# Low parts of three weight units summed by the matrix engine, one softmax in two blocks, taps for two groups at once, and a new order

## The chip, the cores and the metric

The kernel runs on one core of a Trainium2 chip. The metric is device time in microseconds (us). PE is the matrix engine (PEld its weight loads), DVE the vector engine, ACT the scalar engine, POOL the GpSimd engine and SP the engine that issues every DMA here. Each engine works through its own queue in program order and stops at an instruction whose inputs, or whose place to write to, aren't ready.

## The reference, cut to what matters

```python
# q, k, v: (8, 8, 576, 64); nine chunks of 64 keys per sequence
scores = scale * (q_c @ k_c.T)                      # within a chunk
attn = exp(scores - max(scores)); attn = attn / (sum(attn) + 1e-9)
x = (attn @ v_c)                                    # laid out as (8, 576, 512)
gate_pre[t] = sum over k of conv_w[k] * x[t - 4 + k]   # five taps along the sequence, causal
gate = 1 / (1 + exp(-gate_pre))
out = (gate * (x @ w_val)) @ w_out
```

The two weight matrices and the taps arrive as 64-bit floats. All sums are kept near float32 precision: each factor of the two large products is split in a high part and a low part (float32r, the one-pass format of PE), and a product is high·high + high·low + low·high.

## The kernel before, in words

The 4608 tokens are cut in nine groups of 512; groups 0 to 7 hold one sequence's first 512 tokens each and group 8 the last 64 of all eight. Channels stand on the partitions, 512 channels in four tiles of 128. A *pair* (g, p) is one half of a group's heads; its tiles are 128 x 1024.

The string `ORDER` lists the work piece by piece, and every piece is a short function that issues one to 64 instructions. They stand in each engine's queue in that order; nothing else schedules them. All go through the helper `run` (line 130), so the profile shows one line for all; the tiles tell them apart. `SLOTS` lists which buffer each new tile takes (`z`: 38 of 128 x 1024; `b`: four PSUM tiles of 128 x 2 x 512; `e`: two for exponentials). A piece that takes a buffer waits until everything that read its former content is done.

The pieces that matter here:

- `lq`, `lk`, `lv`, `lw`, `lc`: loads (SP). A `w_val` *unit* (`v 0` to `v 3`) is 256 rows by 256 columns, 512 KB.
- `w1` to `w8`, `wa`, `wb`: from 64-bit words to parts. `w1`, `w3`, `w4`, `w7` (DVE), `w2`, `w5` (ACT) pick exponent, sign and mantissa; `wq` is then the leading float32 of a weight and `wr` (made by `w8`, POOL, or `w8D`, DVE) the rest. `w6` (ACT) rounds `wq` to the high part `v_hi`; `wa` computes `wq - v_hi` and `wb` adds `wr`, which gives the low part `v_lo`. A `D` at a name's end moves a piece to DVE.
- `S` (PE): scores of one half (b) of a pair, 16 products of 64 x 64, into PSUM. `mx` (DVE): row maxima. Then either `sb`, `ex`, `sm` (subtract on DVE, one exponential of 128 x 1024 on ACT, sum and reciprocal on DVE) or `ng`, `ea`, `rc`: `ea` is 16 exponentials of 128 x 64 on ACT, with the maximum as bias, each followed by the read of its sum.
- `nm` (POOL): multiply by the reciprocal. `T` (PE): eight transposes by the identity. `ec` (ACT): copy from PSUM. `A` (PE): weighted sum of v. `xr` (ACT): high part of x; `xd` (DVE): low part; `xc` (ACT): x itself.
- `V g m c t` (PE): one term of x·w_val, 512 columns, for output tile m and input tile c (c = 2, 3 belong to pair 1; c = 2 is its first half, c = 3 its second). Term 0 is high·high, 1 uses `v_lo`, 2 the low part of x. `vc` copies the result.
- `k0` (ACT), `k` (DVE): the first and the other four taps, 128 x 512 each. `sg` (ACT): sigmoid. `gs` (DVE): gate times value; `gr` (ACT), `gd` (POOL or DVE): its high and low part. `P g t c` (PE): three terms of the last product. `oc`, `st`: copy and store.
- `W n` (PE): n products of zeros, 128 x 512, that nobody reads; they keep PE busy before its real work is there.

The program opens with the loads, the four `w_val` units and the softmax of the pairs (0, 1), (0, 0) and (1, 0). PE's long work starts with the first `V`, which needs x of pair (0, 1).

Of the kernel before, what the change touches and what calls it, by code (L numbers as in the profile page):

```python
# [66 lines left out]
sg 3 1,k 3 1 4,V 7 3 1,k 6 1 1,P 4 3 1,sg 3 0,k 6 3 3,V 6 0 3,gs 3 1,P 4 1 3,vc 6 0,V 7 3 0,nmD 8 1,P 4 1 2,P 4 3 2,k 7 0 1,
V 7 2 3,k 7 1 2,gs 3 0,P 4 0 2,vc 7 1,P 4 0 3,k0D 5 2,gr 3 1,P 4 1 1,nmD 8 0,gr 3 0,P 4 1 0,k 6 2 2,P 4 3 0,gd 3 0,P 4 0 1,
T 8 1,oc 4 0,T 8 0,ecD 8 1,hc 6 0,P 4 2 2,hc 3 0,gd 3 1,ecD 8 0,P 4 2 3,P 3 2 0,oc 4 1,A 8 0,k0 7 3,hc 7 0,k0D 5 3,hc 5 1,
hc 6 1,hc 0 0,k 5 0 2,A 8 1,hc 4 1,hc 7 1,xr 8 0,hc 5 0,k 6 3 4,P 3 2 1,xc 8 1,xd 8 0,P 3 3 0,k 6 1 2,P 3 3 3,xc 8 0,  # L70
V 8 0 0,k 6 1 3,hb 0,P 3 2 3,hb 1,k 7 3 1,k0 8 2,V 8 1 0,k 6 1 4,xr 8 1,k 6 2 3,V 7 0 0,sg 6 0,xd 8 1,V 7 1 3,P 3 3 1,
k0 8 3,k 8 2 1,P 3 2 2,k 5 0 3,P 3 3 2,k0D 8 0,V 8 0 3,k 6 2 4,oc 3 1,k 5 3 1,V 7 0 1,k0 8 1,k 7 3 2,P 3 0 0,sg 6 1,k 5 0 4,
P 3 0 3,k 5 2 1,V 8 2 0,gs 6 1,P 3 1 2,P 3 1 3,k 5 2 2,gr 6 1,P 3 1 0,k 7 1 3,V 8 2 1,k 5 1 4,P 3 1 1,k 7 0 2,sg 5 0,
# [22 lines left out]
    b="0 0 1 1 2 0 2 2 1 2 1 3 1 0 2 1 1 0 2 1 2 3 3 0 2 1 0 1 0 2 1 0 1 3 1 0 0 1 3 2 0 2 0 0 2 1 3 0 2 2 0 1 3 0 2 "  # L96
      "1 2 2 0 2 1 3 1 0 2 2 2 1 1 0 3 0 2 3 1 3 0 2 3 1 3 1 0 2 1 3 0 3 2 0 1 3 1 0 1 2 3 1",
    e="0 1 1 1 1 0 1 0 1 0 1 0 1 0 1 0 0 1",
)


@with_exitstack
def chunk_attention_gated_conv(ctx, tc, q, k, v, w_val, conv_w, w_out, out):
# [5 lines left out]
    P = 128  # L109
# [417 lines left out]
```

## Time and profile before

| | |
|---|---|
| three runs | 282.32, 285.37, 285.33 us; median 285.33 |
| the profiled execution | 282.82 us, of which the span from first to last instruction is 281.0 |
| busy, share of the span | PE 96%, DVE 87%, PEld 77%, ACT 71%, POOL 23% |
| granted PE clock, mean | 0.994 |
| moved by DMA | 42.47 MB, mean 151 GB/s; some 400 GB/s over the first 60 us |
| chain that ended last | PE 92%, DMA 4%, ACT 2% |

Busy times say how long an engine had an instruction in work, and PE's are modelled where they overlap; the start-to-start distance of neighbours in the timeline is the better price of one. The chain that ended last is followed back from the last instruction, at each step to what released it.

### The profile page before, as it was taken

The page shows a single profiled execution, that of the slowest core. Times are in us where ns is not written, and L with a number is a line of the kernel's source. Part 1 is how long each engine was busy: PE and PEld are TensorE (multiplying, and loading weights), DVE is VectorE, ACT ScalarE, POOL GpSimd, SP SyncE. Part 2 cuts the span into 40 slices and gives each one's busy share as a digit, 9 for nine tenths or more (in the row PEclk, how much of TensorE's full clock was granted, in tenths as well). Part 3 has the DMA queues.
Part 4 walks back from the last instruction along what each step waited for, and adds up shares of the span by engine and source line. Part 5 has one row for each costly group of instructions (what it writes and reads, how often), then busy time and mean ns, then how long its engine had stood idle before and what let it go on. Part 6 is the DMA issues. An engine that isn't in the chain of part 4 may idle for free.

```text
span 281.0 us, 7884 instructions
## 1 busy us (share of the span) xinstructions
PE 270.3 (96%) x3358; PEld 216.2 (77%) x3358; DVE 244.9 (87%) x335; ACT 200.2 (71%) x390; POOL 63.7 (23%) x58
## 2 busy tenths in 40 slices
PE   6498999999999999999999999999999999999995
PEld 2256787887888888888888888888888888887885
DVE  3998999998999798999997999989799999999301
ACT  3686999999889897798798778795595524625011
POOL 1225520461530049160250001100630000210000
PEclk9979999999999999999999999999999999999999
DMA  7999999992010595029055000000000000072156
GB/s 237 355 411 410 409 406 407 378 363 82 9 69 0 204 348 203 3 89 364 2 184 195 0 2 5 0 0 0 2 3 0 0 2 1 0 286 90 77 201 245
DMA packets 15267, 42.47 MB, mean 151 GB/s; under 512 B 1536, under 2 KB 1792, under 8 KB 15232
## 3 DMA queue, kind: packets, MB, share of 16 engines
q1 hardware_dynamic: 15232, 41.97, 39.8%
q8 instruction: 26, 0.43, 0.6%
q14 instruction: 9, 0.07, 0.1%
HBM read 32.53 MB, written 9.44 MB: 149 GB/s over the span
## 4 chain that ended last, share of the span: by engine, by line
PE 92%; DMA 4%; ACT 2%; issue 1%; SPq 0%; ACTq 0%
PE b L130 92%; DMA z<-in_k 3%; DMA z<-in_moe_w_val 2%; ACT z L130 2%; SPq L130 0%; ACTq L130 0%
## 5 line engine op out<-in xcount | busy, mean ns | idle before, releaser
L130 ACT COPY z<-b 128x1024 f32<-128x1024 f32 (+1 forms) x64 | 63.4, 1006 | 50.4 <-PE b L130 50.1
L130 PE MATMUL b<-z,v_hi 128*128 128x512 f32 x288 | 97.4, 401 | 0.1
L130 PE MATMUL b<-o_hi,z 128*128 128x512 f32 (+1 forms) x296 | 96.5, 392 | 0.0
L130 DVE SCALAR_TENSOR_TENSOR z<-z,cw,z 128x509 f32<-128x509 f32 (+3 forms) x128 | 88.6, 743 | 0.1
L130 PEld LDWEIGHTS b<-o_hi,z 128*128 128x128 f32 x296 | 55.1, 188 | 12.5
L130 PEld LDWEIGHTS b<-z,v_hi 128*128 128x128 f32 x288 | 53.9, 188 | 13.4 <-ACT z L130 0.7
L130 PE MATMUL b<-o_lo,z 128*128 128x512 f32 (+1 forms) x148 | 57.5, 388 | 0.0
L130 PE MATMUL b<-z,v_lo 128*128 128x512 f32 x144 | 56.1, 395 | 0.0
L130 PEld LDWEIGHTS b<-z,z 64*64 64x64 f32 x2304 | 36.2, 135 | 15.3 <-issue 9.4
L130 PE MATMUL b<-z,z 64*64 64x64 f32 x2304 | 39.7, 220 | 6.3 <-DMA z<-in_k 3.0
L130 POOL TENSOR_TENSOR z<-z,z 128x1024 fp32r<-128x1024 f32 (+1 forms) x10 | 21.0, 2103 | 101.1 <-ACT z L130 95.4
L130 DVE TENSOR_TENSOR z<-z,z 128x1024 f32<-128x1024 f32 (+2 forms) x33 | 37.0, 1138 | 2.2 <-ACT z L130 1.7
L130 POOL TENSOR_TENSOR z<-e_row,rs 128x1024 f32<-128x1024 f32 x13 | 24.7, 1906 | 55.1 <-DVE rs L130 36.1
L130 ACT ACTIVATE z<-z 128x1024 f32<-128x1024 f32 (+2 forms) x33 | 28.8, 892 | 10.5 <-DVE z L130 10.4
L130 PEld LDWEIGHTS b<-o_lo,z 128*128 128x128 f32 x148 | 27.8, 188 | 5.7
L130 PEld LDWEIGHTS b<-z,v_lo 128*128 128x128 f32 x144 | 27.1, 188 | 5.6
L130 ACT ACTIVATE e_row<-b,mx 128x64 f32<-128x64 f32 x96 | 28.6, 359 | 3.5 <-DVE cw_r L130 2.4
L130 DVE TENSOR_TENSOR z<-b,z 128x1024 fp32r<-128x1024 f32 (+1 forms) x19 | 23.0, 1219 | 3.6 <-ACT z L130 3.4
L130 ACT ACTIVATION_READ_ACCUMULATOR e_row<-b,mx 128x1 f32 x96 | 24.1, 251 | 0.0
L130 ACT CAST z<-z 128x1024 fp32r<-128x1024 f32 x18 | 18.7, 1047 | 5.8 <-DVE z L130 4.8
L130 DVE TENSOR_REDUCE mx<-b 128x16 f32<-128x1024 f32 x18 | 21.3, 1194 | 0.0
L130 DVE COPY z<-b 128x1024 f32<-128x1024 f32 (+2 forms) x8 | 7.8, 989 | 15.2 <-PE b L130 15.2
(50 smaller groups left out, 221.1 us busy)
## 6 DMA issues: line engine op xcount, KB each, us to landing
z<-in_v SPq DMA_DIRECT2D x18, 512.0 KB, 8.3
z<-in_q SPq DMA_DIRECT2D x16, 512.0 KB, 9.9
z<-in_k SPq DMA_DIRECT2D x16, 512.0 KB, 8.4
out<-z SPq DMA_DIRECT2D x16, 512.0 KB, 3.8
z<-in_moe_w_val SPq DMA_DIRECT2D x4, 512.0 KB, 6.2
z<-in_moe_w_out SPq DMA_DIRECT2D x4, 512.0 KB, 10.6
z<-in_k SPq DMA_DIRECT2D x4, 256.0 KB, 6.3
z<-in_q SPq DMA_DIRECT2D x4, 256.0 KB, 6.0
```

The costliest lines, as they stand in the source:

```text
L130: return tc.keep_in_program_order(fn(*args, **kwargs))
```

## The change

**Low parts on PE.** For the units v 1, v 3 and v 2 a piece `Q` (three PE products into PSUM: identity times `wq`, minus identity times `v_hi`, identity times `wr`) and a piece `wc` (ACT copy that rounds to `v_lo`) take the place of `wa` and `wb`. Unit v 0 keeps `wa` and `wb`. A new tile `signed` holds plus and minus identity; ACT fills it (`zs`).

**Two blocks.** For pair (0, 1) the halves of the scores have a PSUM tile each, and `mx`, `ng`, `ea`, `rc`, `nm`, `T`, `ec`, `A`, `xr`, `xd`, `xc` run for one half and then for the other, with half the elements (eight exponentials each instead of 16).

**Two groups at once.** Buffers 20 to 37 become one tile `ys`, so that two of them can be addressed with one stride. `kk` applies a tap to two neighbouring groups in one DVE instruction of 128 x 2 x 508 to 511 (24 of them, for groups 4 with 5 and 6 with 7), `kx` the first tap.

**Fillers.** `W 9 25` (nine products of 512 columns and 25 of 64) at the start replaces `W 14`, `W 7`, `W 9`, `W 1` and `W 3`.

**Order.** The unit v 1 is loaded first and v 3, v 2 ahead of the first k and q; nearly every piece has another place; the buffers are assigned anew.

```diff
-ORDER = """zw,lw v 3,zr 0,zr 1,lw v 1,lc,lk 0 1 0,lq 0 1 0,lq 0 1 1,lk 0 1 1,lw v 2,w1 v 3,...
+ORDER = """zw,lw v 1,zr 1,zr 0,lc,zi,zs 0,zs 1,lw v 3,lw v 2,lk 0 1 0,lq 0 1 0,lq 0 1 1,lk 0 1 1,lq 0 0 0,w1 v 1,...
...
+ALONE = 20
...
+    ys = pool.tile([P, 1 + max(int(i) for i in SLOTS["z"].split()) - ALONE, 2 * T], F32, name="ys")
...
+    signed = pool.tile([P, 2, P], F32R, name="signed")
...
+    def wq_sum(n, c):
+        w_ps[n, c] = unit(bank()[:, 0], n)
+        for i, (lhsT, rhs) in enumerate(((ident, wq[n, c].bitcast(F32)), (signed[:, 1], kept_in(wh, n, c)),
+                                         (signed[:, 0], wr[n, c].bitcast(F32R)))):
+            run(E.matmul, w_ps[n, c], lhsT=lhsT, rhs=rhs if i == 1 else unit(rhs, n), start=i == 0, stop=i == 2)
+
+    def wc(n, c, copy=S.copy):
+        run(copy, out=kept_in(wl, n, c), in_=w_ps[n, c])
...
     def sc(g, p, b):
-        if b == 0:
-            s_ps[g, p] = bank().rearrange("p h (b c k) -> p h b c k", b=2, c=4)
+        own = (g, p) in HALVES
+        if own or b == 0:
+            ps = bank().rearrange("p h (b c k) -> p h b c k", b=2, c=4)
+            if own:
+                s_ps[g, p, b] = ps[:, :, 0]
+            else:
+                s_ps[g, p] = ps
...
+    def ea(g, p, b=None):
+        e = e_of(g, p, b)
+        rss[g, p, b] = r = count("rs")
+        s, m = scores(g, p, b), mxs[g, p, b]
+        for j in range(16 if b is None else 8):
+            eo, si = (e[:, j], s[:, j]) if b is None else (e[:, j // 4, j % 4], s[:, j // 4, j % 4])
+            run(S.activation, out=eo, in_=si, func=AF.Exp, bias=m[:, j:j + 1], scale=SCALE, accum_out=r[:, j:j + 1])
...
+    def two(at, g, hp, a, b):
+        i, j = sorted((at[g, hp // 2][0], at[g + 1, hp // 2][0]))
+        c = hp % 2 * T
+        return ys[:, i - ALONE:j + 1 - ALONE:j - i, c + a:c + b]
...
+    def kk(g, hp, j):
+        d, e = step(xs_at, g, hp // 2), step(acc_at, g, hp // 2)
+        if d * e < 0:
+            tap(g, hp, j)
+            tap(g + 1, hp, j)
+            return
+        a, x = two(acc_at, g, hp, j, T), two(xs_at, g, hp, 0, T - j)
         run(V.scalar_tensor_tensor, out=a, in0=x, scalar=cw[:, hp, TAPS - 1 - j:TAPS - j], in1=a, op0=ALU.mult, op1=ALU.add)
...
-    def keep_warm(n):
+    def keep_warm(n, short=0):
         ps = bank()
-        for _ in range(n):
-            run(E.matmul, ps[:, 0], lhsT=warm[:, :P], rhs=warm, start=True, stop=True)
+        for i in range(n + short):
+            c = slice(0, T if i < n else D)
+            run(E.matmul, ps[:, 0, c], lhsT=warm[:, :P], rhs=warm[:, c], start=True, stop=True)
```

Three places of the queues are spoken of below. First PE's queue up to its first `V` (the rows with `v_hi` or `v_lo` and a z tile, which holds the high part of x). Before, behind `T 0 1` and three fillers, `A` of pair (0, 1) is the row with `z_182`, `T` of (0, 0) the row with `ident`:

```order
L130 MATMUL b_343<-z_333,z_182 64x64 x32
L130 MATMUL b_389<-ident,z_384 128x128 x8
L130 MATMUL b_403<-z_386,v_hi 128x512
L130 MATMUL b_403<-z_386,v_lo 128x512 x2
L130 MATMUL b_403<-z_386,v_hi 128x512 x3
L130 MATMUL b_415<-z_406,z_378 64x64 x32
L130 MATMUL b_452<-z_184,z_376 64x64 x32
```

And in the change, where the rows with `ident` and 128x512 or `signed` are `Q` of v 3 and v 2, `b_309` is `T` of the two halves of (0, 1) with `S 1 0` between them, `b_366` and `b_388` are `A` of the halves:

```order
L139 MATMUL b_291<-z_118,signed 128x512
L139 MATMUL b_299<-z_163,ident 128x512
L139 MATMUL b_299<-v_hi,signed 128x512
L139 MATMUL b_299<-z_168,signed 128x512
L139 MATMUL b_309<-ident,z_297 128x128 x4
L139 MATMUL b_317<-z_192,z_198 64x64 x32
L139 MATMUL b_309<-ident,z_297 128x128 x4
L139 MATMUL b_366<-z_335,z_203 64x64 x16
L139 MATMUL b_388<-z_335,z_203 64x64 x16
L139 MATMUL b_409<-ident,z_383 128x128 x8
L139 MATMUL b_423<-z_386,v_hi 128x512
L139 MATMUL b_425<-z_386,v_hi 128x512
```

The same pairs' pieces stand ahead of the first `V` in both; the fillers between them are gone, and two `Q` stand ahead of the first transposes. PSUM tile number 2 serves `S 0 0`, then `T 0 1`, then `A` of the second half.

Second, ACT's queue from the exponentials of (0, 1) on. Before:

```order
L130 ACTIVATE e_row_63,rs_194<-b_126,mx_180 128x64 x16
L130 CAST v_hi<-z_192 128x2x256
L130 ACTIVATE z_266<-z_88 128x512
L130 ACTIVATE z_299<-z_149 128x512
L130 ACTIVATE z_259<-z_259 128x512
L130 ACTIVATE e_row_64<-e_row_64 128x16x64
L130 COPY z_333<-b_321 128x1024
L130 CAST z_386<-b_343 128x2x2x256
L130 COPY z_400<-b_343 128x2x2x256
L130 COPY z_406<-b_389 128x1024
```

In the change, with `COPY z_335<-b_309` for `ec` of a half, `CAST v_lo` for `wc` and `CAST z_386` for `xr` of a half:

```order
L139 ACTIVATE e_row_65,rs_281<-b_205,mx_236 128x64 x8
L139 ACTIVATE e_row_66<-e_row_66 128x16x64
L139 COPY z_335<-b_309 128x512
L139 CAST v_lo<-b_291 128x2x256
L139 ACTIVATE z_306<-z_306 128x512
L139 CAST v_lo<-b_299 128x2x256
L139 COPY z_335<-b_309 128x512
L139 CAST z_386<-b_366 128x512
L139 COPY ys<-b_366 128x512
L139 ACTIVATE z_407<-z_194 128x512
L139 CAST z_386<-b_388 128x512
L139 COPY ys<-b_388 128x512
```

Between the first `ec` and the first `xr` there was nothing; now two `wc`, a `w2` and the second `ec` stand there, and the copy of `T 0 0` (`ec 0 0`) comes behind all rows shown.

Third, DVE's queue near the end, where the two-group taps stand (rows with 128x2x):

```order
L139 TENSOR_TENSOR z_2989<-ys,z_2979 128x1024
L139 SCALAR_TENSOR_TENSOR ys<-ys,cw 128x2x509 x2
L139 SCALAR_TENSOR_TENSOR z_2842<-tails_74,cw,z_2842 128x512
L139 SCALAR_TENSOR_TENSOR ys<-ys,cw 128x2x509 x2
L139 SCALAR_TENSOR_TENSOR ys<-ys,cw 128x2x508 x3
L139 TENSOR_TENSOR z_3044<-ys,z_2916 128x1024
```

Before, the taps of single groups stood there:

```order
L130 TENSOR_TENSOR z_3096<-z_2645,z_3038 128x1024
L130 SCALAR_TENSOR_TENSOR z_2802<-z_2241,cw,z_2802 128x509
L130 SCALAR_TENSOR_TENSOR z_2677<-z_2531,cw,z_2677 128x510
L130 SCALAR_TENSOR_TENSOR z_2802<-z_2241,cw,z_2802 128x508
L130 SCALAR_TENSOR_TENSOR z_2671<-z_2628,cw,z_2671 128x508
```

All 24 `kk` are one instruction each: the rows with 128x2x508 to 128x2x511 number 24, and those of a single group fell from 128 to 80.

More of the change, by code (lines that the diff above doesn't have):

```diff
@@ L283, in ea, with blocks @@
-    def ea(g, p):
-        probs[g, p] = e_rows[int(next(slots["e"]))]
-        rss[g, p] = r = count("rs")
-        s, m = flat(s_ps[g, p]), mxs[g, p]
-        for j in range(16):
-            run(S.activation, out=probs[g, p][:, j, 0:D], in_=s[:, j], func=AF.Exp, bias=m[:, j:j + 1], scale=SCALE,
-                accum_out=r[:, j:j + 1])
-    def rc(g, p):
-        r = rss[g, p]
+    def blocks(a, b):
+        return a if b is None else a.rearrange("p (h b c) k -> p h b c k", h=2, b=2)[:, :, b]
@@ new lines, in scores, with stat, wide, cols @@
+    def scores(g, p, b):
+        return s_ps[g, p].rearrange("p h b c k -> p (h b c) k") if b is None else s_ps[g, p, b]
+    def stat(a, b):
+        return a if b is None else a[:, 0:8].rearrange("p (h c) -> p h c", h=2)
+    def wide(a, b):
+        return a.unsqueeze(2).broadcast_to([P, 16, D]) if b is None else stat(a, b).unsqueeze(3).broadcast_to([P, 2, 4, D])
+    def cols(a, b):
+        return a if b is None else a[:, 0:8]
+    def mx(g, p, b=None):
+        mxs[g, p, b] = count("mx")
+        run(V.tensor_reduce, out=stat(mxs[g, p, b], b), in_=scores(g, p, b), op=ALU.max, axis=AX.X)
@@ new lines, in e_of, with sb, ex, sm @@
+    def e_of(g, p, b):
+        if not b:
+            probs[g, p] = e_rows[int(next(slots["e"]))]
+        return blocks(probs[g, p][:, :, 0:D], b)
+    def sb(g, p, b=None):
+        run(V.tensor_tensor, out=e_of(g, p, b), in0=scores(g, p, b), in1=wide(mxs[g, p, b], b), op=ALU.subtract)
+    def ex(g, p, b=None):
+        e = blocks(probs[g, p][:, :, 0:D], b)
+        run(S.activation, out=e, in_=e, func=AF.Exp, scale=SCALE)
+    def sm(g, p, b=None):
+        rss[g, p, b] = r = count("rs")
+        run(V.tensor_reduce, out=stat(r, b), in_=blocks(probs[g, p], b), op=ALU.add, axis=AX.X)
+        run(V.reciprocal, out=cols(r, b), in_=cols(r, b))
@@ L293, in rc @@
+    def rc(g, p, b=None):
+        r = cols(rss[g, p, b], b)
         run(V.tensor_scalar, out=r, in0=r, scalar1=1e-9, scalar2=None, op0=ALU.add)
         run(V.reciprocal, out=r, in_=r)
-    def nm(g, p, on=G):
-        normed[g, p] = z().rearrange("p (b k) -> p b k", k=D)
-        run(on.tensor_tensor, out=normed[g, p], in0=probs[g, p][:, :, 0:D], in1=wide(rss[g, p]), op=ALU.mult)
-    def tr(g, p):
-        et_ps[g, p] = bank()
-        to = et_ps[g, p].rearrange("p h (j q) -> p (h j) q", q=P)
-        for j in range(8):
-            run(E.transpose, out=to[:, j, :], in_=normed[g, p][:, 2 * j:2 * j + 2, :].rearrange("p b k -> p (b k)"), identity=ident)
@@ L306, in ec, with nm, tr @@
-    def ec(g, p, copy=S.copy):
-        probs_t[g, p] = z()
-        run(copy, out=twin(probs_t[g, p]), in_=et_ps[g, p])
-    def av(g, p):
-        et = probs_t[g, p].rearrange("p (h b a q) -> p h b a q", h=2, b=2, a=2)
+    def nm(g, p, b=None, on=G):
+        if not b:
+            normed[g, p] = z().rearrange("p (b k) -> p b k", k=D)
+        run(on.tensor_tensor, out=blocks(normed[g, p], b), in0=blocks(probs[g, p][:, :, 0:D], b), in1=wide(rss[g, p, b], b), op=ALU.mult)
+    def tr(g, p, b=None):
+        if not b:
+            et_ps[g, p] = bank()
+        to = et_ps[g, p].rearrange("p h (j q) -> p (h j) q", q=P)
+        for h in range(2):
+            for f in range(2) if b is None else (b,):
+                for a in range(2):
+                    j = 4 * h + 2 * f + a
+                    run(E.transpose, out=to[:, j if b is None else 4 * f + 2 * h + a, :],
+                        in_=normed[g, p][:, 2 * j:2 * j + 2, :].rearrange("p b k -> p (b k)"), identity=ident)
@@ L312, in av, with ec @@
+    def ec(g, p, b=None, copy=S.copy):
+        if not b:
+            probs_t[g, p] = z()
+        if b is None:
+            run(copy, out=twin(probs_t[g, p]), in_=et_ps[g, p])
+        else:
+            run(copy, out=twin(probs_t[g, p])[:, b], in_=et_ps[g, p][:, b])
+    def av(g, p, own=None):
+        et = probs_t[g, p].rearrange("p (h b a q) -> p h b a q" if own is None else "p (b h a q) -> p h b a q", h=2, b=2, a=2)
         vv = vt[g, p].rearrange("p (b h a w d) -> p b h a w d", b=2, h=2, a=2, w=2)
-        x_ps[g, p] = bank()
@@ L452, in zi, with zs_ @@
         make_identity(nc, ident)
+    def zs_(i):
+        run(S.mul, signed[:, i], ident, 1.0 - 2.0 * i)
     def zw():
```

263 lines of the change are left out of this document (140 added, 123 removed), and 12 rows, old and new, of the table z.

## The prediction

> **What bounds the kernel now.** I read the chain of work that ended last first, in order of time (start, length, what). Its longer pieces from 13.8 us on are nearly all PE's:
>
> ```profile
> 13.78 6.14 PE b L130 x135
> 25.15 1.95 ACT z L130 x2
> 27.14 37.07 PE b L130 x795
> 64.21 0.70 issue
> 64.91 12.94 PE b L130 x87
> 79.27 198.80 PE b L130 x2158
> ```
>
> From 27.1 us to 278.1 us PE waits for 0.70 us in one place and about 1.4 us around 78 us in the chain's terms, where PE itself shows hardly a gap. The second view is the timeline of PE at the program's start (start, length, instruction, count, idle before):
>
> ```profile
> 9.15 0.69 PE L130 MATMUL b<-z,z 64*64 64x64 f32 x32 [0.64 <-DMA z<-in_k]
> 9.78 1.68 PE L130 MATMUL b<-warm 128*128 128x512 bf16 x7
> 13.78 1.51 PE L130 MATMUL b<-z,z 64*64 64x64 f32 x64 [2.32 <-DMA z<-in_k]
> 15.22 3.61 PE L130 MATMUL b<-warm 128*128 128x512 bf16 x9
> 20.80 1.06 PE L130 MATMUL b<-ident,z 128*128 128x128 f32 x8
> 25.31 0.50 PE L130 MATMUL b<-z,v_hi 128*128 128x512 f32 x1
> 27.14 2.10 PE L130 MATMUL b<-z,z 64*64 64x64 f32 x128 [0.16 <-ACT z L130]
> 29.17 0.50 PE L130 MATMUL b<-z,v_hi 128*128 128x512 f32 x1
> 36.72 1.78 PE L130 MATMUL b<-z,v_hi 128*128 128x512 f32 x7
> ```
>
> The first `V` stands at 25.31; neighbours of this kind then come every 0.23 us (1.78 us less one overlap, over seven). So the time is made of three things: the start up to the first `V`, some 252 us of dense PE work, and 2.9 us of last copy and store behind 278.1. The change leaves the real PE work behind the first `V` as it is: the same pieces stand ahead of it in both, and the number of products is equal. What it can win is the start, and what it can lose are new waits later. The third view, busy time by stretch (PE, PEld, DVE, ACT, POOL, clock), says who could make PE wait:
>
> ```profile
> 40.00:60.00 20.00, 20.00 (x445) 16.29 (x447) 19.34 (x29) 19.66 (x50) 6.97 (x4) 1.00 1.01 391
> 80.00:100.00 20.00, 20.00 (x240) 16.44 (x229) 18.41 (x29) 18.59 (x50) 3.73 (x3) 1.00 0.28 105
> 240.00:260.00 20.00, 20.00 (x88) 16.08 (x87) 19.35 (x20) 10.05 (x10) 2.68 (x1) 1.00 0.35 132
> 260.00:270.00 10.00, 10.00 (x46) 8.19 (x45) 2.72 (x3) 1.02 (x1) 0.00 (x0) 1.00 0.41 157
> ```
>
> DVE is almost as full as PE up to 260 us, and ACT up to 60. A start that is shorter by x pulls every later date of DVE forward by x too.
>
> **The start, step by step.** The rows for it, DVE, ACT and POOL:
>
> ```profile
> 10.16 1.22 DVE L130 TENSOR_REDUCE mx<-b 128x16 f32<-128x1024 f32 x1
> 18.39 1.23 DVE L130 TENSOR_TENSOR e_row<-b,mx 128x1024 f32<-128x1024 f32 x1
> 20.73 1.24 DVE L130 TENSOR_REDUCE rs<-e_row 128x16 f32<-128x1040 f32 x1
> 11.69 0.32 ACT L130 ACTIVATE e_row<-b,mx 128x64 f32<-128x64 f32 x1 [2.40 <-DVE cw_r L130]
> 16.24 0.30 ACT L130 ACTIVATION_READ_ACCUMULATOR e_row<-b,mx 128x1 f32 x1
> 19.64 1.06 ACT L130 ACTIVATE e_row<-e_row 128x1024 f32<-128x1024 f32 x1 [0.96 <-DVE e_row L130]
> 21.95 1.01 ACT L130 COPY z<-b 128x1024 f32<-128x1024 f32 x1 [1.25 <-PE b L130]
> 24.24 1.01 ACT L130 CAST z<-b 128x1024 fp32r<-128x1024 f32 x1 [1.28 <-PE b L130]
> 26.96 0.64 ACT L130 CAST v_hi<-z 128x512 fp32r<-128x512 f32 x1
> 17.42 1.91 POOL L130 TENSOR_TENSOR z<-e_row,rs 128x1024 f32<-128x1024 f32 x1 [6.05 <-DVE rs L130]
> 24.04 1.27 POOL L130 TENSOR_TENSOR z<-z,z 128x512 f32<-128x512 f32 x1 [1.81 <-DMA z<-in_moe_w_out]
> ```
>
> Sixteen exponentials take 11.69 to 16.54, 0.29 us per step, so eight take 2.3. For a half block I take 0.6 of DVE's 1.22, 1.0 of POOL's 1.91 and 0.55 of ACT's 1.01; a half can't cost more than the whole, so each lies between half a row and a row, and the half plus a little is nearest to the 0.64 us of a 128x512 cast.
>
> - Loads: 512 KB more of weights stand ahead of the first k and q. Between PE's starts at 9.15 and 13.78, 1.5 MB landed, 3.1 us per MB, so the second half of the scores starts at about 10.7 instead of 9.15; the first at about 9.3. What `S 0 0` needs is the same number of bytes as before: 13.7.
> - First half: maxima from 10.1 (DVE is through with two units' bits then), exponentials 11.0 to 13.3. Second half behind one cast: 13.9 to 16.2, against 16.54 before. Splitting saves little there, since ACT does the same 16.
> - DVE next does maxima and subtraction of (0, 0), 14.9 to 17.2 (its scores come at 14.8), then the second reciprocal at 18.0. POOL: the rest of v 2 (1.27) to 14.6, first multiply to 15.6, second 18.1 to 19.1.
> - First transposes: their PSUM tile holds the scores of (0, 0) until 17.2. So they end at about 17.7 if PE is there, against 21.9 before.
> - ACT in its new order: the exponential of (0, 0) 17.3 to 18.35, `ec` 18.9, `wc` 19.45, `w2` 20.0, `wc` 20.6, second `ec` 21.1, `xr` 21.7. Against 25.25 before, where `T`, `ec`, `A`, `xr` followed each other for the whole pair.
> - The sum of (0, 0) on DVE 18.45 to 19.95, its multiply on POOL to 21.9 (before it was on DVE), its transposes to 22.9. They stand ahead of the first `V`, which so starts at about 22.9: **2.4 us earlier.**
> - Then five `V` (1.2 us) until 24.1; `A 0 0` needs `ec 0 0`, which ACT reaches behind `xc`, `w5`, second `xr` and `xc`: 23.85 to 24.8. PE stalls 0.8 us (0.16 before). `A 0 0` and `S 1 1` then end at 26.95, against 29.17 before, with five `V` done instead of six: **2.0 us gained**, if PE's `Q` are out of the way in time.
>
> **What Q costs.** The trace has no 128x512 product in plain float32. The nearest row is the transpose: eight of 128 columns in 1.06 us less an overlap of 0.25, 0.10 us for 128 columns, so 0.41 us for 512; and every 64x64 product of the program is two PE instructions (2304 for 1152 in the queue), so up to 0.81. With two one-pass products of 0.23 a `Q` is 0.87 to 1.3 us; I take 1.3. The Trainium skill, FP8 and Floating Point Precision, section TensorE Precision Notes, counts four passes for true FP32; with 0.23 us per pass that would be an estimate of 0.93 + 0.46 = 1.4 us. `Q` of v 1 is done in PE's idle time at 7 us. Those of v 3 and v 2 stand behind `S 0 0` (14.8): to 17.4 at full clock, just in time for 17.2 above. What they take off DVE and POOL (two `wb`, one `wa` on DVE, 0.6 us each as half of a 1.22 row, three of 1.3 on POOL) is paid by `wc`, 0.55 each, on ACT, where it lies between `ec` and `xr`; it is in the dates above.
>
> But the clock isn't full there. Granted clock by microsecond (PE busy, count, clock, DMA):
>
> ```profile
> 12.00:13.00 1.00, 0.00 (x0) 1.00 1.05 406
> 15.00:16.00 1.00, 1.00 (x13) 0.50 1.02 408
> 17.00:18.00 1.00, 1.00 (x4) 0.50 1.10 438
> 18.00:19.00 1.00, 1.00 (x17) 0.85 0.97 389
> ```
>
> PE idled from 11.46 to 13.78, and from about 14.9 to 18.3 the clock was half: nine fillers took 3.61 us (0.40 each) where seven took 1.68 (0.24), which is 1.45 us lost, on fillers alone. In the change the idle time at 8 to 13.7 us is longer, for the fillers at 9.78 are gone, and the half clock falls on `Q` of v 3 and v 2: 2.6 us each. If it lasts until 18.3, the first is done at 18.5, the second at 19.8, the transposes at 20.3. ACT stands at `ec` from 18.35, and all behind it moves by 2.0 us: **nothing is left of the 2.0.** Whether the gate falls on `Q` depends on where its period lies; I take half of the loss, so a gain of 1.0 with bounds 0 and 2.0.
>
> The rule on this is the Trainium skill's TensorE: Matmul & The Clock Gate, section Part 1: after an idle window of some 3.4 us the clock is halved, a busy one restores it, and the window runs free of the program. The trace agrees: half clock for about 3.4 us. By it the removal of 25 long fillers is a risk, a rival below.
>
> **Later.** Behind `S 1 1` I added up the queues to the first gate products of group 1, since there DVE is nearest. From the sum of (1, 0), which ends at 27.45 by the dates above, to `gdD 1 0` DVE has 39 taps (0.67), 27 instructions of 1024 columns (1.16 apart), four sums with reciprocal (1.5), 22 of 512 columns (0.36 to 0.61) and 7 small ones: 75.1 us. PE has, from 26.95 to `P 1 0 0`, 235 products (0.2325), 8 `T` (0.85), 6 `A` (1.09) and 14 halves of `S` (0.55): 75.7, and 1% for changing between kinds, 76.6. So DVE is there at 102.5, PE at 103.5. To `gdD 1 1` it is 109.2 against 110.0 by the same count. That leaves 0.8 to 1.0 us for all of DVE's waits on the way. In the row 80 to 100 above DVE is idle 1.6 us of 20, so PE will wait; before, the tightest of these places left
>
> ```profile
> 122.02 2.42 POOL L130 TENSOR_TENSOR z<-z,z 128x1024 fp32r<-128x1024 f32 x1 [8.42 <-ACT z L130]
> 124.71 0.50 PE L130 MATMUL b<-o_hi,z 128*128 128x512 f32 x1
> ```
>
> 0.27 us. Bounds of a new stall: 0 and 3.5 (all that DVE idled between 30 and 100 us); I take 1.0, for half of that idling was DVE waiting for PE. The old stall of 0.70 counts as half removed, 0.4.
>
> **Two groups at once** is priced at nothing. Rows for it:
>
> ```profile
> 113.74 5.36 DVE L130 SCALAR_TENSOR_TENSOR z<-z,cw,z 128x511 f32<-128x511 f32 x8
> L130 DVE TENSOR_TENSOR z<-z,z 128x1024 f32<-128x1024 f32 x17 | 20.6, 1221 | 0.9 <-ACT z L130 0.9
> ```
>
> Two taps cost 1.34 us, one instruction of twice the length 1.14 to 1.34 (the second row less the overlap of neighbours). At most 24 x 0.2 = 4.8 us go off DVE, all in groups 4 to 7. There PE is the bound, and DVE is done by 260 us with PE's last 18 us still to come, so this is only slack. If an odd stride cost more than two taps, that slack covers some 5 us. The tail is unchanged: the last store is again 128 KB behind a 128x256 copy.
>
> **Sum**, on the profiled execution: 282.82 - 1.0 (start) - 0.4 (old stall) + 1.0 (new stalls at the gates) = 282.4. Two of the three runs lie 2.5 us above that execution, which one trace can't explain; I add half of that spread: **283.6 us**, against the median of 285.33. A difference under 2% (5.7 us) is about what a measurement of this kernel can't tell from no change.
>
> **Rivals**, on the same scale (before would be 284.1 on it):
>
> - *The start is kept in full.* `Q` run at full clock and DVE, with less to do for the units, is in time: -2.0 - 0.9 and no new stall, 281.2. For it speaks that DVE and POOL lose six instructions at the start; against it the half clock in the rows.
> - *The clock makes it slower.* Without fillers PE is busy for little more than half of 18.3 to 22.9, so the clock falls again and the first `V` run at half: another 1.45 us as for the nine fillers, nothing gained at the start, and 1.0 at the gates: 284.1 + 2.45 = 286.5. It decides once the clock's low stretch reaches past 22.9. By the skill's clock-gate rule this needs a window that counts as idle; the trace shows one with 2.3 us of idling, none with less.
> - *DVE paces groups 1 and 2.* All 3.5 us of its idling come back as PE stalls before 125 us: 284.1 - 1.4 + 3.5 = 286.2. For it: 0.27 us before. Against: half of that idling was caused by PE.
> - *The two-group taps aren't joined* (the code falls back to two taps when the buffers' strides have opposite signs): the queue shows all 24 joined, so no chance is given to it.
>
> **How the numbers follow.** Forecast 0.5, full gain 0.2, clock 0.17, DVE 0.13. The unknown costs move the forecast by -2.4 to +2.5 and the runs' spread by 1.3 either way; with the rivals the range is 279.5 to 287.5. Faster by over 2% (below 279.6) needs the full gain and a low run: 0.1. Slower by over 2% (above 291.0) needs clock and DVE together: 0.06. Within 2%: 0.84.
>
> **What would show it.** The first `V` between 22.9 and 25.3 us; the half clock on a product with `ident` of 128x512, and the first `ec` late by as much; a gap of PE before its products of group 1; DVE's taps of 2 x 509 at 1.14 to 1.34 us; the last product 2.9 us before the end. A first `V` before 22, PE stalls of over 3 us in one place, or a PE gap after 130 us would prove me wrong.

## The result and the profile after

The changed kernel took 287.81 us, median of 7 runs (286.48 to 288.78); the kernel before beside it 283.82 (282.32 to 285.37). The ratio is 1.0129, 95% interval 1.0086 to 1.0173: **slower by 1.3%, 4.0 us**. Six more runs (`e11_after`, below) gave 287.18 against 283.85, 1.0112 (1.0069 to 1.0155). The forecast was 283.6, range 279.5 to 287.5, so it was wrong in sign, and the time lies just out of its range. The profiled execution took 287.81 us, its span 286.0 against 281.0 before.

The start came near the forecast. PE's timeline of the changed kernel (start, length, instruction, count, idle before):

```profile
15.33 2.08 PE L139 MATMUL b<-z,ident 128*128 128x512 f32 x2
17.86 1.02 PE L139 MATMUL b<-z,ident 128*128 128x512 f32 x2
19.19 0.60 PE L139 MATMUL b<-ident,z 128*128 128x128 f32 x4
24.09 0.80 PE L139 MATMUL b<-z,v_hi 128*128 128x512 f32 x2
26.05 2.10 PE L139 MATMUL b<-z,z 64*64 64x64 f32 x128 [0.46 <-ACT z L139]
28.07 1.20 PE L139 MATMUL b<-z,v_hi 128*128 128x512 f32 x4
```

The first `V` stands at 24.09 instead of 25.31; `S 1 1` is through at 28.07 instead of 29.17 with one `V` fewer done: 1.10 less 0.23, 0.87 us gained. The loss stands in the middle of the program, in the first half of `S 4 0`. The chain of work that ended last, 60 to 70 us, and PE's rows there:

```profile
60.81 4.06 PE b L139 x147
64.87 2.91 issue
67.78 2.56 PE b L139 x54
```

```profile
64.42 0.45 PE L139 MATMUL b<-ys 64*64 64x64 f32 x13
67.78 1.03 PE L139 MATMUL b<-ys 64*64 64x64 f32 x51 [2.91 <-issue]
68.74 0.74 PE L139 MATMUL b<-z,v_hi 128*128 128x512 f32 x1
72.73 0.39 PE L139 MATMUL b<-z,v_lo 128*128 128x512 f32 x1
```

PE stands still for 2.91 us between the 13th and the 14th of 64 products of one kind, waiting for nothing that the profile shows. Before, that was 0.70 us at 64.21, also inside `S 4 0`. Then ten `V` take from 68.74 to 72.73, 3.99 us; in the kernel before, the ten behind the same scores took 2.44 (65.53 to 67.97), which makes 1.55 us lost. The windows give the reason for that loss (PE, PEld, DVE, ACT, POOL, clock, DMA share, GB/s):

```profile
64.00:66.00 2.00, 0.87 (x16) 0.37 (x14) 1.92 (x3) 1.97 (x3) 1.14 (x1) 1.00 0.97 391
66.00:68.00 2.00, 0.22 (x12) 0.22 (x16) 0.00 (x0) 2.00 (x3) 1.92 (x3) 1.00 0.19 70
68.00:70.00 2.00, 2.00 (x54) 1.75 (x47) 1.15 (x2) 1.39 (x3) 0.72 (x1) 0.71 0.16 25
70.00:72.00 2.00, 2.00 (x6) 1.54 (x6) 1.97 (x4) 0.81 (x1) 0.33 (x1) 0.50 0.62 236
```

The granted clock falls to half behind the gap. PE's other new waits stand in the list of who waited for whom (total, times, longest):

```profile
PE b L139 <- issue: 2.9, 1, 2.9
PE b L139 <- ACT z L139: 1.2, 3, 0.6
PE b L139 <- DVE z L139: 0.6, 1, 0.6
PE b L139 <- PE b L139: 0.4, 1, 0.4
```

Behind the start these are 0.40 us that end at 60.81 (a PSUM buffer), 0.62 that end at 126.45 (ACT) and 0.63 that end at 164.09 (DVE), each absent before. So, against before: -0.87 start, +2.21 the longer gap, +1.55 half clock, +1.65 the three waits: +4.54 of the 5.0 us between the spans; 0.46 stays unexplained.

**What PE waited for.** The page's list of DMA queues has one that moves neither inputs nor outputs:

```profile
q1 hardware_dynamic: 15232, 41.97, 39.9%
q8 instruction: 26, 0.43, 0.6%
```

There are 26 packets of 16.4 KB, as before. Windows of 0.1 us show when one moves. Here are the window from 65.4 us of the changed kernel, and that from 62.6 us of the one before:

```profile
q1 hardware_dynamic: 10, 0.04, 90.0%
q8 instruction: 1, 0.02, 62.5%
```

```profile
q8 instruction: 1, 0.02, 60.0%
q1 hardware_dynamic: 3, 0.01, 30.2%
```

PE goes on 2.4 us behind the first (67.78) and 2.3 us behind the second (64.91). So I read q8 as PE's own program: a packet is a block of some 128 products with their weight loads. The gaps lie after 1105 and 1107 products, counted from the program's start with the fillers. One block earlier, at product 977, PE was at 61.15; that is when the fetch would have begun. The packet came 4.25 us later, and in between the DMA engines were busy with five loads of 512 KB: k of (4,1), issued at 56.76, and the four that SP issues next:

```profile
57.13 0.93 SPq L139 DMA_DIRECT2D ys<-in_v  x1
58.16 0.37 SPq L139 DMA_DIRECT2D z<-in_v  x1
58.70 0.33 SPq L139 DMA_DIRECT2D ys<-in_q  x1
59.12 0.55 SPq L139 DMA_DIRECT2D ys<-in_v  x1
```

The kernel before also has five loads there, but it issues the first four from 54.38 to 57.23. From PE's entry into the block until the loads have drained, 1.23 MB of them moved there (59.8 to 63.7 us) and 1.81 MB in the changed kernel (61.1 to 67.0); in both, the packet comes near the loads' end.

Behind the gap itself, with DMA nearly idle, the next packet moves at 68.9, 1.1 us after PE went on. The experiments test three theories: "fetch" (the block is late behind the loads), "burst" (small products use up the program too fast, loads or not) and "place" (something that `S 4 0` itself waits for).

The Trainium skill, Runtime: NRT & Kernel Launch, section Instruction fetch mechanics, says that a sequencer refills its instructions in 16 KiB blocks of 256 through a DMA queue of its own, and that crossing a block is mostly hidden. The packets of 16.4 KB agree with the first; the 2.91 us do not agree with the second.

### The profile page after: what moved, and what is told of

Same layout as the page of the kernel before. It is cut to its first block, busy times and chain, and to the rows that moved or that the text cites. A ratio compares the mean times of both kernels' runs of the same rounds, so it can differ in the third digit from the quotient of the medians.

```text
span 286.0 us, 7887 instructions
## 1 busy us (share of the span) xinstructions
PE 272.0 (95%) x3370; PEld 219.4 (77%) x3370; DVE 242.0 (85%) x309; ACT 198.3 (69%) x392; POOL 63.3 (22%) x59
## 4 chain that ended last, share of the span: by engine, by line
PE 68%; DVE 15%; DMA 8%; ACT 3%; issue 3%; SPq 1%; DVEq 0%; ACTq 0%
PE b L139 68%; DVE ys L139 10%; DMA z<-in_q 3%; DMA out<-z 3%; DVE z L139 3%; DMA z<-in_moe_w_val 2%; ACT z L139 2%; SPq L139 1%; DVE mx L139 1%; ACT ys L139 1%; DVE e_row L139 1%; ACT L139 0%; DVE o_lo L139 0%; ACT v_lo L139 0%; DVE rs L139 0%
## 5 line engine op out<-in xcount | busy, mean ns | idle before, releaser
L139 DVE SCALAR_TENSOR_TENSOR ys<-ys,cw 128x511 f32<-128x511 f32 (+7 forms) x104 | 85.0, 865 | 0.1
L139 ACT COPY z<-b 128x1024 f32<-128x1024 f32 (+2 forms) x49 | 46.8, 974 | 49.9 <-PE b L139 49.4
L139 POOL TENSOR_TENSOR z<-e_row,rs 128x1024 f32<-128x1024 f32 (+1 forms) x17 | 31.6, 1857 | 57.7 <-DVE rs L139 46.6
L139 POOL TENSOR_TENSOR z<-ys,z 128x1024 fp32r<-128x1024 f32 x5 | 12.0, 2409 | 73.9 <-ACT z L139 66.3
L139 PEld LDWEIGHTS b<-z,z 64*64 64x64 f32 x1216 | 20.9, 141 | 8.9 <-issue 2.9
L139 PE MATMUL b<-z,z 64*64 64x64 f32 x1216 | 23.5, 228 | 4.4 <-DMA z<-in_q 2.1
L139 DVE TENSOR_REDUCE mx<-b 128x16 f32<-128x1024 f32 (+1 forms) x19 | 21.9, 1151 | 4.7 <-PE b L139 4.6
L139 ACT CAST z<-ys 128x1024 fp32r<-128x1024 f32 x16 | 16.6, 1045 | 11.0 <-DVE ys L139 10.9
L139 PE MATMUL b<-ident,z 128*128 128x128 f32 x144 | 19.2, 275 | 0.8 <-DVE z L139 0.6
L139 ACT CAST z<-b 128x1024 fp32r<-128x1024 f32 (+1 forms) x19 | 18.6, 981 | 1.7 <-PE b L139 1.6
```

The source lines that it names most:

```text
L139: return tc.keep_in_program_order(fn(*args, **kwargs))
```

## The experiments

### Loads held back

`e1_hold` adds one instruction to ACT, and with it a wait to the first of the five loads.

```diff
+    def hold(which, g, p):
+        kept = {"lq": qt, "lk": kt, "lv": vt}[which]
+        kept[g, p] = z()
+        run(S.copy, out=kept[g, p][:, 0:1], in_=ident[:, 0:1])
-V 2 1 2,gr 0 0,sm 3 0
+V 2 1 2,gr 0 0,hold lk 4 1,sm 3 0
```

> The changed kernel, but five loads of 512 KB (k of (4,1) first, and the four behind it in the queue) are held back from about 57 us to about 68 us by a one-column write of ACT into the first one's buffer; PE's program is the same. Theory 'fetch' (PE's program comes in blocks through a DMA queue, and the block that PE needed at 64.87 us landed only at 65.4 us because it stood among these loads; the clock then fell because PE stood still): the block's packet lands within 1.5 us of 61.2, PE's gap at 64.9 us is 0 to 0.5 us instead of 2.91, the clock stays 1.00 from 18 us on, and the time falls by 3.5 to 4.7 us from the changed kernel's 287.8, to 283.1 to 284.3. Theory 'burst' (small products use up the program faster than it can come, whatever the loads do): the gap stays at 2.5 to 3 us, 287.8. Theory 'place' (something that this group of scores itself waits for): gap and time stay, 287.8.

Measured: 284.84 us, ratio to before 1.0062 (1.0037 to 1.0087). The packet moves at 63.3 us, 1.1 us after PE entered the block (62.25), and `S 4 0` runs through in one piece:

```profile
65.62 1.44 PE L137 MATMUL b<-ys 64*64 64x64 f32 x64
```

The clock stays 1.00 behind it. So this gap goes with the loads: "fetch" holds; "place" falls, and so does "burst" as the cause of this gap. The time falls by less than I expected, 3.0 us between the medians (1.9 by the ratios), since in the profiled execution the sums of v 3 and v 2 both ran at half clock and the first `V` starts at 25.30 instead of 24.09: nothing was left of the start. The held loads also made `S 4 1` 0.38 us late at 79.7.

### The same program, 16 products or 40 further on

`e2_plus16` is the changed kernel with `W 9 41` for `W 9 25`. `e4_before40` is the kernel before with `W 14 40` for `W 14` (its `W` gets the second number, as in the changed one).

> The changed kernel with 41 short filler products at its start instead of 25; all else is the same. Theory 'fetch': the block's boundary lies 16 products earlier in the program, so the gap leaves the scores of (4,0) and stands ahead of the last three or so products of the gate before them, at about 63.7 us; as the packet comes at about the same time (65.1 to 65.4, PE 2.4 us later), the gap grows from 2.9 to 3.5 to 4.1 us, the clock falls behind it as before, and the time is 0.3 to 1.2 us longer than 287.8: 288.1 to 289.0. Theory 'burst': the same shift, the gap of any size. Theory 'place': the gap stays behind the 13th product of the scores of (4,0), 2.9 us, 287.8.

> The kernel before with 40 short filler products (128x64) behind its first 14, where PE waits for q anyway; all else as before. Theory 'fetch': the boundary that costs 0.70 us at 64.2 us moves 40 products ahead, to about 61.9 us, where PE reaches it 2.7 us after the block's start instead of 4.35; with the packet as late as before (5.05 us from block start to go) the gap is 1.8 to 2.8 us, and the time is 1.1 to 2.1 us longer than the kernel before's, up to 3.6 if the clock falls too. Theory 'burst': a gap of that sort as well. Theory 'place': the gap stays 0.70 in its group of scores, no difference in time (under 0.4 us).

Measured: 294.30 us, ratio 1.0427 (1.0354 to 1.0500), and 293.01 us, 1.0341 (1.0285 to 1.0397). **Sixteen tiny products, done where PE has nothing else to do, cost 6.5 us between the medians (6.9 when each is taken against the kernel before measured beside it); forty cost the kernel before 9.6 us.** PE's rows of `e2_plus16` and of `e4_before40`:

```profile
68.12 0.39 PE L138 MATMUL b<-z,v_hi 128*128 128x512 f32 x1
71.61 0.39 PE L138 MATMUL b<-z,v_hi 128*128 128x512 f32 x1 [3.10 <-issue]
...
173.38 1.16 PE L138 MATMUL b<-z,z 64*64 64x64 f32 x64
174.36 0.99 PE L138 MATMUL b<-z,ys 64*64 64x64 f32 x55
176.82 0.38 PE L138 MATMUL b<-z,ys 64*64 64x64 f32 x9 [1.47 <-issue]
```

```profile
31.95 0.49 PE L130 MATMUL b<-z,z 64*64 64x64 f32 x6 [2.88 <-issue]
...
70.70 0.62 PE L130 MATMUL b<-z,v_hi 128*128 128x512 f32 x2 [3.18 <-issue]
```

The gap has left `S 4 0` in both and lies among `V`, again after 1105 and 1104 products from the start: it belongs to a place in the count, not to an operation. That is what "fetch" said. The times I had far too small, for I had looked at one boundary: in `e2_plus16` the gap there is 3.10 us, less than the 3.5 to 4.1 I expected and without half clock behind it, but three other boundaries have gaps too (2.31, 1.53, 1.47; together 8.41 against 2.91), and `e4_before40` has three of over 1 us (2.88, 3.18, 1.38). The four gaps of `e2_plus16` and the later one of `e3_moved` (below) begin after 473, 1105, 1486, 2120 and 2756 products: 5, 3, 5 and 5 times 126 to 127 apart, so a block is about that long. The gap that ends at 176.82 has no loads before it (DMA share 0.00 from 168 to 174 us and 0.04 from 174 to 176): there two `A` in a row take PE through 119 products in 1.97 us. So "burst" is a cause too, and needs no load.

### Loads moved to a place without a gap

`e3_moved` takes four loads out of 44 to 59 us:

```diff
-lq 7 0,lk 7 0,lk 4 1,lv 3 1,lv 4 1,lq 6 0,lv 3 0
+lk 4 1,lv 3 1,lv 3 0
-sm 4 0,k0 2 2,S 4 1 1
+sm 4 0,k0 2 2,hold lq 7 0,lq 7 0,lk 7 0,lv 4 1,lq 6 0,S 4 1 1
```

> The changed kernel with four loads of 512 KB (q and k of (7,0), v of (4,1), q of (6,0)) moved from 44 to 59 us to about 79 to 84 us, where DMA is idle and PE runs through two blocks in 3.6 to 3.9 us each without a gap; the first of them is held by a one-column write of ACT behind the first tap of (2,2). Theory 'fetch': the gap at 64.9 us shrinks to 0 to 0.8 us, and a new one of 1 to 3.5 us shows up between 78 and 88 us, in the products that had none, with its packet over 2.5 us behind the block's start, and half clock behind it if it is longer than about 2.5 us; the time is 283.5 to 287.5. Theory 'burst': the gap at 64.9 stays at 2.9 and none appears at 78 to 88; 287.8. Theory 'place': as 'burst'.

Measured: 285.78 us, 1.0083 (1.0060 to 1.0106). PE's rows at the old place and at the new one:

```profile
66.12 1.03 PE L137 MATMUL b<-ys 64*64 64x64 f32 x51 [0.16 <-issue]
```

```profile
88.12 0.50 PE L137 MATMUL b<-o_lo,z 128*128 128x512 f32 x1 [1.15 <-issue]
```

The old gap is 0.16 us, and a new one stands where the loads went, in products that had none; there the clock stays 1.00. Time and gaps are as "fetch" said.

### The smallest repair, and the changed kernel again

`e10_order` changes the order of three loads, without any added wait: `lv 3 0,lq 4 1,lv 4 1,lq 6 0` for `lv 4 1,lq 6 0,lv 3 0,lq 4 1`. `e11_after` is the changed kernel again, measured beside it.

> The changed kernel with v of (4,1) and q of (6,0) loaded behind q of (4,1), nothing else: q of (4,1) waits for its buffer until about 69 us, so three loads of 512 KB instead of five stand before PE's block of program. Theory 'fetch': its packet lands at 63.4 to 64.2 us instead of 65.4, PE's gap at 64.9 us is 0 to 1.2 us instead of 2.91, no half clock behind it, and the time is 1.8 to 3.5 us under the changed kernel's in the same call. 'Burst' and 'place': the gap stays at 2.9 us and the time equal within 0.5 us.

> The changed kernel itself once more, beside the one before and on the same chip, for the size of the difference: 286.5 to 288.5 us, a ratio of 1.009 to 1.017; PE's gap of 2.4 to 3.2 us at 64 to 66 us is there again (theory 'fetch'), with half clock behind it or without.

Measured: 284.83 us, 1.0021 (0.9994 to 1.0047), and 287.18 us, 1.0112 (1.0069 to 1.0155): 2.4 us between the medians. PE's rows of the one and the other:

```profile
66.45 1.03 PE L137 MATMUL b<-ys 64*64 64x64 f32 x51 [0.99 <-issue]
```

```profile
66.93 1.07 PE L139 MATMUL b<-ys 64*64 64x64 f32 x51 [2.42 <-issue]
```

Behind the second, half clock (0.50 from 68 to 70 us); behind the first, 1.00. Over all these runs, PE goes on at nearly one distance from the packet:

| kernel | packet in the 0.1 us from | PE goes on | apart | gap |
|---|---|---|---|---|
| before | 62.6 | 64.91 | 2.3 | 0.70 |
| changed | 65.4 | 67.78 | 2.4 | 2.91 |
| changed, again | 64.6 | 66.93 | 2.3 | 2.42 |
| `e10_order` | 64.0 | 66.45 | 2.4 | 0.99 |
| `e2_plus16` | 30.5 / 69.3 / 137.3 / 174.1 | 32.90 / 71.61 / 139.57 / 176.82 | 2.4 / 2.3 / 2.3 / 2.7 | 2.31 / 3.10 / 1.53 / 1.47 |
| `e3_moved` | 63.8 / 85.7 | 66.12 / 88.12 | 2.3 / 2.4 | 0.16 / 1.15 |
| `e4_before40` | 29.4 / 68.2 / 175.5 | 31.95 / 70.70 / 177.88 | 2.5 / 2.5 / 2.4 | 2.88 / 3.18 / 1.38 |

Thirteen of thirteen lie between 2.3 and 2.7; three small gaps that the table leaves out (0.21 in `e10_order`, 0.35 in `e7_small`, 0.40 in `e8_both`) do too. With 1.1 us from a block's start to its packet when DMA is idle, a block needs some 3.5 us to be ready; in a run without such gaps (`e5_start`) packets come as close as 3.50 and 3.56 us, and in none of these traces closer than 3.34. So PE has a gap when it has done a block's 128 products in less than these 3.5 us plus the packet's delay behind loads; the gap is the rest.

### The clock at the start

`e5_start` is `e1_hold` with its 34 fillers spread over PE's idle time, the count ahead of later pieces unchanged.

```diff
-W 9 25,Q v 1 ... S 0 1 0 ... S 0 1 1 ... S 0 0 0 ... S 0 0 1
+W 9 11,Q v 1,W 7 ... S 0 1 0,W 2 ... S 0 1 1,W 2 ... S 0 0 0,W 2 ... S 0 0 1,W 1
```

> The held-loads kernel (284.84 us) with its 34 fillers spread: 20 at the start as before it, 7 long ones behind the summed unit v 1, then 2, 2, 2 and 1 behind the four pieces of the first two scores, all in PE's idle time; the number of PE's instructions ahead of every later piece is the same. Theory 'clock' (the start loses its gain because PE idles between 8 and 15 us and runs the two sums of v 3 and v 2 at half clock, 2.7 and 2.3 us each in that run): the clock stays 1.00 to 20 us, each sum takes 1.3 us, the first product of the gate starts at 23.3 to 24.3 us instead of 25.3, and the time falls by 0.7 to 1.6 us, to 283.2 to 284.1. Rival 'chain of the softmax' (DMA, ACT and DVE set the start, PE only looks on): the first gate product stays at 24.9 or later and the time within 0.4 us of 284.84.

Measured: 283.89 us, 1.0003 (0.9978 to 1.0028). PE's rows and the windows:

```profile
15.66 1.02 PE L137 MATMUL b<-z,ident 128*128 128x512 f32 x2
16.99 1.02 PE L137 MATMUL b<-z,ident 128*128 128x512 f32 x2
19.10 0.63 PE L137 MATMUL b<-ident,z 128*128 128x128 f32 x4 [0.64 <-DVE e_row L137]
23.86 1.09 PE L137 MATMUL b<-ident,z 128*128 128x128 f32 x8 [0.61 <-POOL z L137]
24.71 0.72 PE L137 MATMUL b<-z,v_hi 128*128 128x512 f32 x2
```

```profile
12.00:14.00 2.00, 1.75 (x66) 1.24 (x66) 1.97 (x7) 1.46 (x11) 0.00 (x0) 1.00 1.03 401
16.00:18.00 2.00, 2.00 (x7) 1.10 (x6) 1.93 (x4) 1.93 (x14) 1.39 (x2) 1.00 1.02 400
```

The clock stays full and a `Q` takes 1.33 us start to start. The time falls by 0.95 us between the medians (1.7 by the ratios), as "clock" said, to the kernel before's. But the first `V` is at 24.71, later than expected, for now the transposes wait for DVE's subtraction of (0,0) and then for POOL: the rival has its share.

### Single taps, small waits, and a version of all

`e6_single` does each two-group tap as two (`if True:` for `if d * e < 0:` in both places) on `e1_hold`.

> The held-loads kernel (284.84 us) with every two-group tap and two-group first tap done as two single ones, in the same places. My theory (prices 1.27 us for one of two groups, 2 x 0.70 for two single ones, all of it under PE): DVE is busy 2 to 4 us longer, PE's waits for DVE at 150.8 and 159.8 us (0.40 and 0.64 us) grow by 0 to 0.6 us together, the time is the same within 0.7 us: 284.4 to 285.5. Rival 'the joined taps hold up what stands behind them on DVE' (they are twice as long, so a short piece that PE needs waits longer): those two waits fall to under 0.2 us each and the time falls by 0.6 to 1.0 us, to 283.9 to 284.2.

Measured: 285.23 us, 1.0062 (1.0036 to 1.0089), the ratio of `e1_hold`. DVE is busy 245.8 us against 243.1; PE's waits for it that end at 150.48 and 160.43 us are 0.21 and 0.63. Joining the taps is worth nothing in time, as forecast.

`e7_small` moves two `V` products ahead of `A 0 0`, `V 5 2 0` ahead of `T 7 1` and `A 5 0` ahead of `T 6 0`; `e8_both` does so on `e5_start`.

> The held-loads kernel (284.84 us) with PE's order changed in three places: two gate products ahead of the weighted sum of (0,0), one gate piece (three products) ahead of the transposes of (7,1), and the weighted sum of (5,0) ahead of the transposes of (6,0). Theory 'small waits' (what is left of the loss, behind the late block of program, are PE's short waits for ACT and DVE: 0.54 at 26 us, 0.40 at 151, 0.64 at 160): each of the three falls under 0.15 us and the time falls by 1.0 to 1.6 us, to 283.2 to 283.8. Rival 'given back later' (DVE or ACT paces, so the wait moves to the next piece): the same sum of waits stands within 10 us behind, and the time stays within 0.5 us of 284.84.

> Held loads, spread fillers and the three swaps together. If 'clock' and 'small waits' both hold, their gains add: 1.7 to 3.0 us below 284.84, so 281.8 to 283.1, at or under the kernel before (283.42 in the last runs). If the start is not on the path or the waits move, 283.4 to 284.8.

Measured: 285.32 us, 1.0024 (0.9988 to 1.0060), and 284.57 us, 1.0019 (0.9995 to 1.0043). The first is inconclusive: two of the three waits are gone, the third became one for ACT (0.59, to 151.43), and a block's boundary cost 0.35 at 33.45; the median is no lower than that of `e1_hold` and above the forecast, while the intervals of the two ratios overlap. The second misses: it is no faster than `e5_start`. Its trace shows new gaps:

```profile
32.23 0.51 PE L137 MATMUL b<-z,v_lo 128*128 128x512 f32 x1 [0.40 <-issue]
...
79.07 1.16 PE L137 MATMUL b<-ys 64*64 64x64 f32 x64 [0.99 <-issue]
```

The first is 2.6 us behind a packet: PE came to the block's end sooner than the block. The second is not behind one; there `S 4 1` waits, I take it, for its held q, which `e9_best` loads sooner. It keeps two of the swaps, takes 10 fillers out (`W 9 1`) and has the order of loads of `e10_order`.

> Spread fillers (283.89 us) plus: two of the three swaps (the gate products ahead of the weighted sum of (0,0), the gate piece ahead of the transposes of (7,1)); 10 short fillers fewer, so that PE's block of program that began at 32 us in the last kernel, 0.40 us late, begins 10 gate products later; and v of (4,1) and q of (6,0) loaded behind q of (4,1), so that the scores of (4,1), 0.99 us late at 79 us, have their q 2.6 us sooner. Theory 'fetch and loads': both gaps fall under 0.15 us, the waits at 26 and 160 us too, and the time is 0.6 to 1.8 us under 283.89: 282.1 to 283.3, a ratio to the kernel before of 0.994 to 0.998. Rival 'given back later': DVE, ACT or the block at 61 to 64.5 us (which has no slack left) take the gain, 283.6 to 284.6.

Measured: 283.35 us against 284.31 for the kernel before beside it, 0.9962 (0.9933 to 0.9991), 0.05 us above the time I expected, with the ratio within what I expected. In its list of waits none has "issue" as its reason, and PE's row at the old gap reads

```profile
65.05 1.16 PE L137 MATMUL b<-ys 64*64 64x64 f32 x64
```

So it is 0.4% faster than the kernel before and 1.5 to 1.7% faster than the changed one (0.9962 against 1.0112 and 1.0129).

## Why the prediction was wrong

- **The old stall: the step that failed.** I counted the 0.70 us of "issue" as half removed, -0.4, without a reason, for I had not asked what "issue" was. It was PE waiting for its own program. In the changed kernel more of the five loads was still on its way when PE entered that block, the gap grew to 2.91 us, and half clock came behind it: +2.21 + 1.55 instead of -0.4. `e1_hold` and `e10_order`, which change only the loads' time and order, are 3.0 and 2.4 us faster than the changed kernel between the medians (1.9 and 2.6 by the ratios). The page of the kernel before has q8 in its list of queues, and its windows give DMA shares of 0.98 and 1.05 at 58 to 62 us; I used neither.
- **The start: right in its mechanism, near in size by luck.** -0.87 in the profiled execution for a forecast of -1.0. I had both sums of v 3 and v 2 at half clock or neither, and took half the loss; here the first ran at half and the second at full clock. The phase of the clock decides: with both sums at half clock (`e1_hold`) nothing is left of the gain, and with none (`e5_start`) 0.95 us comes back. The 22.9 us without half clock was too early: DVE's subtraction of (0,0) ended at 17.9 in the changed kernel where I had 17.2, for its scores came later.
- **Q:** 0.87 to 1.3 us, taken at 1.3; measured 1.33 at full clock (17.86 to 19.19) and 2.53 at half (15.33 to 17.86).
- **New waits:** I took 1.0 within 0 and 3.5, at the gates of group 1. There, none came. Three others came, 1.65 us together: that the sum was near is luck, for the place was wrong. My own sign of being wrong, a gap of PE after 130 us, came too (0.63 to 164.09, for DVE): the taps of the late groups are not all slack, as I had it. (1% on 75.7 us makes 76.5, not 76.6; nothing hangs on it.)
- **Two-group taps:** forecast 1.14 to 1.34 us each and no gain in time; both held (`e6_single`). The row of the changed kernel, with the mean of one in ns:

```profile
L139 DVE SCALAR_TENSOR_TENSOR ys<-ys,cw 128x1018 f32<-128x1018 f32 x6 | 7.5, 1276 | 0.0
```

- **The rivals:** none was this one. "The clock makes it slower" named half clock, but at the start. "DVE paces groups 1 and 2" has a share: the chain that ended last runs over DVE for most of 92.0 to 124.4 us, but it cost PE only the 0.62 us to 126.45, not 3.5. I also held a difference under 2% for one that can't be told; the interval came out 0.9% wide.
- **What was left out:** with the late block repaired, `e10_order` has 284.83 us at a ratio of 1.0021 (0.9994 to 1.0047), close to my forecast of hardly any difference. The sum left out one resource, the transfer of PE's own program.

## What to carry to other kernels

A gap of PE in the middle of equal products with "issue" as its reason is a sign that the program comes late: find out when the instruction queue's packet moves and which loads stand before it. An edit that shifts PE's count of instructions, even by fillers in idle time, moves every such boundary and can cost 2 to 3%; keep large loads away from dense groups of small products, and compare versions with the count kept. Fillers that keep PE busy while it waits for loads held the clock here, and are worth what the work behind them loses at half clock.

## What the runs showed of the hardware

- A block of PE's program needs about 3.5 us (1.1 to its packet, 2.3 to 2.7 from there; no two packets of these traces are closer than 3.34), 5.05 behind loads in the kernel before and 6.6 in the changed one (61.15 to 67.78).
- Half clock followed gaps of this sort of 2.31, 2.42, 2.88, 2.91 and 3.18 us, but not one of 3.10 and none of 0.16 to 1.53. What decides between them is where a gap falls. In `e2_plus16` the clock changes at 12.07, 18.90, 32.55 and 35.96 us, which are 2, 4 and 1 times 3.41 us apart. On that grid the gap of 2.31 leaves PE busy for 1.45 us of one window, idle for 1.96, and the next is at half clock; the gap of 3.10 is cut in two, 1.58 us idle in one window and 1.52 in the next, and the clock stays (the columns are as in the first windows above):

```profile
29.14:32.55 3.41, 1.45 (x6) 0.84 (x5) 3.41 (x5) 3.41 (x7) 2.46 (x2) 1.00 1.03 406
66.68:70.09 3.41, 1.83 (x69) 1.48 (x59) 3.41 (x5) 3.39 (x5) 0.52 (x1) 1.00 0.82 326
70.09:73.50 3.41, 1.89 (x68) 1.41 (x67) 0.54 (x1) 2.85 (x4) 3.27 (x3) 1.00 0.06 14
```

- The other four gaps that half clock followed have 1.97 to 2.42 us of idling in one such window. In the first 15 us of the programs the border is less sharp: 1.71 us idle drew half clock in `e1_hold`, and 1.85 in the window before it did not. The Trainium skill, TensorE: Matmul & The Clock Gate, section Part 1, has a window of about 3.4 us that runs free of the program, and half clock after an idle one; the grid agrees with the first, but a window with 1.96 of its 3.41 us idle was enough.
